# A state-space layer and an MLP on one core: the same operations in a newly found order, and one memset in 32-bit words

## The chip, the cores and the metric

The kernel runs on one core of a Trainium2 chip. The metric is the device time of one execution in microseconds (us). The core has a matrix engine (TensorE, "PE" in the profile; its weight loads are shown as "PEld"), a vector engine (VectorE, "DVE"), a scalar engine (ScalarE, "ACT") and a general engine (GpSimd, "POOL"). SyncE ("SP") issues nearly all DMA transfers. Each engine works through its own instructions in the order in which they are written, and waits for others by semaphores. So an instruction that waits holds up all that stands behind it on its engine.

## The reference

```
x  = A_u                                     # 1 x 2048 x 512, bf16
h  = x + A(layernorm(x))                     # state-space convolution
h2 = h + B(layernorm(h))                     # MLP 512 -> 1376 -> 512

A:  dt = exp(log_dt);  logdA = dt*(A_re + i A_im)       # 512 x 128
    K[d, l] = Re sum_n C[d,n] * exp(logdA[d,n]*l) * dt*B[d,n]     # l = 0..2047
    y = irfft(rfft(pad(K)) * rfft(pad(u)))[:2048] + u * Dskip
B:  y = layernorm(x);  gelu(y @ w1 + b1) @ w2 + b2      # with the tanh form of gelu
```

The position `l` is rounded to bf16 in the reference, and the kernel follows that rounding with masks.

## The kernel before

The 2048 positions are two blocks of 1024 (b = 0, 1), the 512 channels four column groups of 128 (c = 0 to 3). The stages, in the order in which the work mostly runs:

- **Front.** GpSimd fills small tables of constants with many small memsets (`fld_fn`, `cv_fn`, `cv3_fn`, `cod_fn`), VectorE and ScalarE make rates, angles and sizes from the parameters (`Front.rates`, `angles`, `size`, `side`, `phase`; helpers `TS`, `STT`, `TT` with lines 565 to 584, ScalarE's `AC` with line 591). `restack` and `phase` send small pieces through DMA to other partitions. This is done for two halves of the channels, c = 0, 1 and c = 2, 3.
- **Tables.** `aexps` and `bexps` make exponentials. `chain` (lines 985 to 1010) and `chain1` (lines 1019 to 1031) keep an angle in PSUM, to which TensorE adds a step; ScalarE takes its sine (lines 1000, 1029), and VectorE multiplies it into the tables EA, EB, IA and IB (lines 1010, 1031).
- **Kernel samples.** `kgen` (lines 1049 to 1068) makes K from the tables of one c by many small matmuls, 33 columns each, in half-groups of 5 or 6 indices. `kspec` and `kspec1` put K into order, write it to DRAM (AK_d for c = 0, 1; AKc_d for c = 2 and c = 3) and read it back in another layout; `fstage` (line 940) makes the spectrum. `ktail` and `klate` do the later half of K through AL_d.
- **Input.** `load_u` brings the input block (eight DMAs of 128 KB each block), `lnorm` normalizes it (bn_stats on line 899, scaling on line 906), `austage` (line 919) and `xspec` transform it.
- **Inverse.** `inverse` multiplies spectra on VectorE (line 1193) and transforms back on TensorE (line 1203). `turn` (line 1219) turns a result over by a DMA transpose on SP; for c = 3 of the first block TensorE does it (line 1212).
- **MLP.** `tail` adds the residual, normalizes twice and turns the result for the MLP (lines 1273 to 1305). `mlp` runs `w1` (line 1321, gelu on ScalarE, line 1323), `w2` (line 1337) and the last add (line 1339) for four pieces of 512 positions, and stores them.

Copies out of PSUM go through `evac` (ScalarE on line 517, VectorE on line 519), and each may be given to either engine. Everything lies in one SBUF arena, so every tile is called `ar` in the profile, and every PSUM tile `ps`.

The code first lists 1094 operations (`Sched.add`, with an engine, a planning cost, what is read and written) and then emits them in the order of the list `ORDER`. An entry k stands for operation k//2, and k%2 says which of its engines runs it. A negative entry -1-z puts one fill matmul on TensorE that writes PSUM bank z and is read by nobody (line 1434, in `fill`). `SLOTS` gives the PSUM banks in the same order. The costs, the `hv` numbers and the functions `c_act` and `c_dve` were used by the planner that found ORDER; when the kernel is built they have no effect. The order of ORDER alone fixes each engine's queue, SP's DMAs included.

Of the kernel before, what the change touches and what calls it, by code (L numbers as in the profile page):

```python
# [13 lines left out]
i32 = mybir.dt.int32  # L14
# [168 lines left out]
class VS(V):  # L183
# [59 lines left out]
]  # L243
SLOTS = "01012012034626026502020244602624062662062604046020262604064202462704264026024602460264206406204602467024602745020120415701425601624024672303642074350501246210675460165323401613712360172314231041502310"


TURN = 450000


class Sched:  # L250
    def __init__(self):
        self.ops = []
        self.wr, self.rd = {}, {}
        self.pr = 0.0
# [82 lines left out]
def c_act(n, ptr=0):  # L337
    return max(0.12, 0.055 + n / 1200.0) + (0.0, 0.09, 0.225, 0.225)[ptr]


def c_dve(n, mode=1, psum=False):
    return (0.08 if n < 64 else 0.065) + n / mode / 960.0
# [3 lines left out]
def kernel(ctx, tc, A_u, A_A_re, A_A_im, A_B_re, A_B_im, A_C_re, A_C_im, A_log_dt, A_Dskip,  # L346
# [4 lines left out]
    class Pe:  # L351
        n, dry, act, md = 0, True, 0.0, []
# [220 lines left out]
    def TT(o, a, b, op, n=None, mode=1, psum=False, oap=None, aap=None, bap=None, pr=None, eng="DVE"):  # L573
# [3 lines left out]
        if op == ALU.pow:  # L577
            c["POOL"] = 0.6 + 0.19 * n
# [907 lines left out]
```

## Time and profile before

| | us |
|---|---|
| median of 3 runs | 243.34 (242.45 to 243.55) |
| the profiled execution, whole time | 245.59 |
| its span, first to last instruction | 243.2 |
| TensorE busy | 215.4 (89%) |
| VectorE busy | 179.6 (74%) |
| ScalarE busy | 170.5 (70%) |
| GpSimd busy | 18.3 (8%) |

The granted clock of TensorE was 0.999 over the span. The chain of work that ended last is 59% TensorE, 26% VectorE, 5% DMA, 4% "issue" (time in which an engine waited for nothing that the profile shows) and 3% SP's queue. A row for a group of instructions gives line, engine, operation, shapes and number, then busy time, the mean of one in ns, and the idle time before them with what ended it. A row of a timeline gives start, length and the same names, with idle time before it in brackets. A row for a stretch of time gives, after its bounds and length, the busy time and the number of instructions for PE, PEld, DVE, ACT and POOL, then the granted clock, the share of the DMA engines' time, and GB/s.

### The profile page before, as it was taken

What the parts mean: (1) busy time and instruction counts of PE and PEld (TensorE: products, weight loads), DVE (VectorE), ACT (ScalarE), POOL (GpSimd) and SP (SyncE); (2) the same over time, 40 slices, a digit from 0 to 9 for tenths busy, and PEclk for the clock granted to TensorE, in tenths of its full rate; (3) what the DMA queues carried; (4) which work ended last, traced back from release to release, by engine and by line L of the source; (5) the groups of instructions that cost most, each with busy time, mean ns of one, the idle gap of its engine ahead of it and who ended that gap; (6) DMA issues with size and microseconds to landing.
All of it is one profiled execution on the core that took longest, in us unless ns stands there. A gap on an engine that the chain in (4) does not pass through costs nothing.

```text
span 243.2 us, 8615 instructions
## 1 busy us (share of the span) xinstructions
PE 215.4 (89%) x3696; PEld 126.2 (52%) x3705; DVE 179.6 (74%) x407; ACT 170.5 (70%) x232; POOL 18.3 (8%) x145
## 2 busy tenths in 40 slices
PE   7559786878988876979998999999999999999994
PEld 2436243656634454755775476655554444444443
DVE  6999999999999995659998988797506991213022
ACT  3999999999999956975997987785134402903700
POOL 8800000011000000300000010010000101000000
PEclk9999999999999999999999999999999999999999
DMA  5121124000013943417899485644514051142303
GB/s 149 34 62 44 38 19 82 20 3 7 3 25 82 214 132 125 125 30 163 231 159 210 121 254 95 214 80 85 99 28 83 0 106 27 41 88 65 86 19 71
DMA packets 42448, 21.40 MB, mean 88 GB/s; under 512 B 30761, under 2 KB 40618, under 8 KB 42410
## 3 DMA queue, kind: packets, MB, share of 16 engines
q1 hardware_dynamic: 42250, 20.79, 38.0%
q8 instruction: 29, 0.48, 0.8%
q10 hardware_dynamic: 160, 0.07, 0.1%
q14 instruction: 9, 0.07, 0.1%
HBM read 10.33 MB, written 4.49 MB: 61 GB/s over the span
## 4 chain that ended last, share of the span: by engine, by line
PE 59%; DVE 26%; DMA 5%; issue 4%; SPq 3%; ACT 1%; DVEq 0%; ACTq 0%
PE ps L1321 16%; PE ps L1337 16%; PE ps L1203 7%; DVE ar L579 5%; DVE ar L519 4%; DMA ar<-ar 4%; PE ps L919 4%; PE ps L940 3%; DVE ar L1010 3%; SPq L530 3%; DVE ar L584 3%; PE ps L1054 3%; DVE ar L1031 3%; PE ps L1278 3%; PE ps L1055 2%
## 5 line engine op out<-in xcount | busy, mean ns | idle before, releaser
L517 ACT CAST ar<-ps 128x1024 bf16<-128x1024 f32 (+4 forms) x66 | 59.0, 941 | 16.7 <-PE ps L1203 7.5
L1323 ACT ACTIVATE ar<-ps,ar 128x512 bf16<-128x512 f32 (+1 forms) x44 | 27.6, 686 | 35.3 <-PE ps L1321 35.3
L1321 PE MATMUL ps<-ar 128*128 128x512 bf16 (+1 forms) x176 | 39.8, 379 | 0.0
L1337 PE MATMUL ps<-ar 128*128 128x512 bf16 (+2 forms) x179 | 38.5, 366 | 0.6 <-issue 0.3
L1339 DVE TENSOR_TENSOR ar<-ps,ar 128x512 bf16<-128x512 f32 (+1 forms) x17 | 10.8, 657 | 36.1 <-PE ps L1337 32.7
L519 DVE CAST ar<-ps 128x1024 bf16<-128x1024 f32 (+5 forms) x29 | 29.2, 1015 | 8.9 <-ACT ar L1029 2.8
L1193 DVE TENSOR_TENSOR ar<-ar 128x1024 bf16<-128x1024 bf16 x48 | 30.7, 685 | 6.5 <-PE ps L1203 6.0
L1337 PEld LDWEIGHTS <-ar 128*128 128x128 bf16 (+1 forms) x187 | 18.0, 98 | 19.6
L1321 PEld LDWEIGHTS <-ar 128*128 128x128 bf16 (+1 forms) x176 | 17.2, 100 | 20.4 <-issue 1.0
L1054 PE MATMUL ps<-ar 128*20 128x33 bf16 x512 | 20.0, 249 | 6.1 <-issue 5.6
L1203 PE MATMUL ps<-ar 64*128 64x128 bf16 x768 | 23.7, 216 | 0.1
L1203 PEld LDWEIGHTS <-ar 64*128 64x128 bf16 x768 | 21.5, 94 | 4.3 <-issue 2.1
L1029 ACT ACTIVATE ar<-ps 128x1024 bf16<-128x1024 int16 x20 | 19.6, 1039 | 3.0 <-issue 2.4
L579 POOL TENSOR_TENSOR ar<-ar 128x4 f32<-128x4 f32 (+1 forms) x6 | 7.4, 1226 | 187.5 <-DVE ar L584 149.3
L1010 DVE TENSOR_TENSOR ar<-ar 128x1024 bf16<-128x1024 bf16 x32 | 21.2, 684 | 0.2
L1055 PEld LDWEIGHTS <-ar 128*20 128x20 bf16 x512 | 17.7, 125 | 6.5 <-issue 6.4
L1055 PE MATMUL ps<-ar 128*20 128x33 bf16 x512 | 20.1, 248 | 0.0
L1054 PEld LDWEIGHTS <-ar 128*20 128x20 bf16 x512 | 17.6, 124 | 3.0 <-DVE ar L1031 1.5
L723 ACT ACTIVATE ar<-ar 128x512 bf16<-128x512 f32 x32 | 18.2, 628 | 0.5 <-DVE ar L565 0.5
L919 PE MATMUL ps<-ar 128*32 128x512 bf16 x256 | 15.7, 380 | 1.4 <-ACT ar L517 0.6
L1027 PE MATMUL ps<-ar 128*32 128x256 f16 (+2 forms) x288 | 13.5, 280 | 2.8 <-ACT ar L1029 2.7
L1031 DVE TENSOR_TENSOR ar<-ar 128x512 bf16<-128x512 bf16 x40 | 15.4, 413 | 0.3
(99 smaller groups left out, 284.6 us busy)
## 6 DMA issues: line engine op xcount, KB each, us to landing
ar<-in_A_u_dram SPq DMA_DIRECT2D x16, 128.0 KB
ar<-in_A_u_dram SPq DMA_DIRECT2D x8, 256.0 KB
out_dram<-ar SPq DMA_DIRECT2D x30, 64.0 KB
ar<-in_B_w_dram SPq DMA_DIRECT2D x4, 344.0 KB
ar<-in_B_w_dram SPq DMA_DIRECT2D x2, 640.0 KB
AK_d<-ar SPq DMA_DIRECT2D x2, 512.0 KB
ar<-AK_d SPq DMA_DIRECT2D x2, 512.0 KB
AKc_d<-ar SPq DMA_DIRECT2D x4, 256.0 KB
```

The costliest lines, as they stand in the source:

```text
L517: act.copy(out_fn(), in_fn())
L519: dve.tensor_copy(out_fn(), in_fn())
L919: pe.matmul(pst(p)[32 * j:32 * j + 32, 512 * z:512 * z + 512], lhsT=BX.ap()[:, f0 + z, 16 - 16 * c:48 - 16 * c], rhs=src[2 * j + c].ap(), ...
L1010: add("DVE", c_dve(1024, 2), lambda e, lo=lo, rv=rv, sz=sc[z], e0=e0, o0=o0, q=q: dve.tensor_tensor(ent(o0, q, lo, 4, rv), ent(e0, q, lo, ...
L1031: add("DVE", c_dve(512, 2), lambda e, sc=sc, b0=b0, tb=tb, z=z: dve.tensor_tensor(tb[b0:b0 + 4].ap(), EA[c][b0:b0 + 4].ap(), sc[z].ap(), A ...
L1054: pe.matmul(o, lhsT=Ar.ap()[:, :, d], rhs=Br.ap()[:, :, d], start=True, stop=False, tile_position=(0, 32 * g))
L1055: pe.matmul(o, lhsT=Ai.ap()[:, :, d], rhs=Bi.ap()[:, :, d], start=False, stop=True, tile_position=(0, 32 * g))
L1193: dve.tensor_tensor(o, a, b_[:, :, ::-1, :] if sw else b_, ALU.mult)
L1203: pe.matmul(pst(p)[:, 512 * h + 128 * k:512 * h + 128 * k + 128], lhsT=q.ap()[rows, 2 * k + r, :], rhs=TP[w].ap()[rows, f0 // 2 + k, :], s ...
L1321: pe.matmul(pst(p)[:fs], lhsT=w1s[dc].ap()[:, fc * P:fc * P + fs], rhs=ybuf.ap().rearrange("p (t c) k -> p c t k", c=4)[:, dc], start=(dc ...
L1323: add("ACT", c_act(512, 1), lambda e, p=p, fc=fc, fs=fs: act.activation(hT.ap()[:fs, fc, :], pst(p)[:fs], ACT.Gelu_apprx_tanh, bias=b1_sb. ...
L1337: pe.matmul(pst(p)[:, c0:c1], lhsT=hT.ap()[:fs, fc, 128 * t:128 * t + 128], rhs=w2s[fc].ap()[:fs, c0:c1], start=(fc == 0), stop=(fc == NFC ...
```

## The change

The operations and their arithmetic stay. One memset of VectorE, of the value 256.0 in 16-bit floats over 2048 elements of one partition, is written as 1024 32-bit words that hold the same bits. Planning costs and `hv` numbers of several operations are altered. ORDER and SLOTS are replaced by newly found ones.

```
-    add("DVE", 0.3, lambda e: dve.memset(HLs.part(64, 65).ap().rearrange("p c g d -> p (c g d)"), 256.0), w=[HLs.part(64, 96)], pr=0.5)
+    add("DVE", 0.95, lambda e: dve.memset(HLs.part(64, 65).ap().rearrange("p c g d -> p (c g d)").bitcast(i32), 0x5C005C00), w=[HLs.part(64, 96)], pr=0.5)

 def c_act(n, ptr=0):
-    return max(0.12, 0.055 + n / 1200.0) + (0.0, 0.09, 0.225, 0.225)[ptr]
+    return max(0.12, 0.1 + n / 1200.0) + (0.0, 0.09, 0.2, 0.2)[ptr]
...
-            c["POOL"] = 0.6 + 0.19 * n
+            c["POOL"] = 0.37 + 0.16 * n
...
 ORDER = [
-    94, 396, 382, 386, 78, 380, 0, 284, 72, 30, 32, 100, 2, 98, 38, 40, 96, 228, 4, 146, 42, 310, 138, 44, 76, 282, 102, 8, 200, 104, 300, 110, 118,
...
-    2136, 2138, 2178, 2180, 2162, 2160, 2148, 2164, 2182, 2166, 2186, 2168, 2170, 2150, 2184, 2172, 2174,
+    0, 78, 94, 310, 386, 30, 32, 384, 382, 96, 100, 2, 38, 98, 4, 146, 228, 68, 8, 6, 40, 198, 312, 138, 300, 54, 102, 266, 314, 302, 12, 104, 118,
...
+    2160, 2138, 2170, 2174, 2136, 2180, 2182, 2172, 2186, 2184,
 ]
-SLOTS = "01012012034626026502020244604262...
+SLOTS = "01232013450262626242240244636404...
```

Decoded, the two orders differ in these places, among others:

| queue | before | after |
|---|---|---|
| SP, start | all six parameter loads and log_dt, one u load, then restacks and u loads mixed | four parameter loads and log_dt, small bias and Dskip loads between the other two, then restacks, most u loads of block 0 behind them |
| SP, middle | 8 u loads of block 1, 2 AK_d writes, AK_d read, AL_d write, AK_d read, AL_d write | 2 AK_d writes, AK_d read, 8 u loads of block 1, AK_d read, 2 AL_d writes |
| SP, next | AL_d reads and 3 loads of x, then 4 AKc_d writes, 4 AKc_d reads, first `turn` | an AL_d read, the first large `w2` load, AL_d reads and 1 load of x among the first two AKc_d writes, 2 AKc_d reads, 2 more writes, first `turn`, 2 more AKc_d reads |
| VectorE, start | 13 operations ahead of the first product of `rates` (line 579) | 10 |
| TensorE, fill matmuls | 11, 8, 6 and 3 ahead of `kgen` for c = 2, 10 in the first `tail` | 8, 6 and 3, and 10 |
| TensorE | last `austage` group of block 0 and a late step of `chain1` behind the first half-groups of `kgen` for c = 2 | ahead of it |
| `lnorm` of block 0 | among the first sines of `chain1` | behind most table products of c = 0, 1 |
| GpSimd | `select` ahead of the large iota of the front | last of the early work |

36 copies and scalings change between ScalarE and VectorE: 19 to VectorE, 17 to ScalarE.

More of the change, by code (lines that the diff above doesn't have):

```diff
@@ L199 @@
 ORDER = [
[43 rows of a table removed]
[43 rows of a table added]
 ]
-SLOTS = "01012012034626026502020244602624062662062604046020262604064202462704264026024602460264206406204602467024602745020120415701425601624024672303642074350501246210675460165323401613712360172314231041502310"
+SLOTS = "01232013450262626242240244636404042626042602602624624202046204622046702460206426042640240264026402640236042364704504675467360247014026452601412632464563701670356071234725360125601205321642405601340102"
 TURN = 450000
@@ L567, in fn @@
                 en.tensor_scalar(a, b, f(s1), f(s2), op0, op1)
-        add(eng, max(c_dve(n, mode, psum), 0.15 if isinstance(s1, V) else 0.0) if eng == "DVE" else 0.25 + n / 1540.0, fn, r=r, w=[o], pr=pr, hv=1)
+        add(eng, max(c_dve(n, mode, psum), 0.15 if isinstance(s1, V) else 0.0) if eng == "DVE" else 0.25 + n / 1540.0, fn, r=r, w=[o], pr=pr, hv=3 if mode == 4 else 2)
     def PTS(o, i, s1, s2=1.0, op0=ALU.mult, op1=ALU.mult, **k):
@@ L638, in fld_fn @@
                 gp.memset(t_.ap()[:, n:n + 1], v_)
-    POOL(2.0, fld_fn, w=[fi, fsh, fmk, fm, fa], pr=0.05, hv=1)
+    POOL(2.0, fld_fn, w=[fi, fsh, fmk, fm, fa], pr=0.05, hv=2)
     TT(fi, fi, fsh, ALU.logical_shift_right, pr=0.1)
@@ L654 @@
     codT = at(X0[8].lo, i32, 16, 2, 64)
-    POOL(1.1, lambda: gp.iota(iT.ap(), pattern=[[4, 16], [64, 64]], base=1, channel_multiplier=0), w=[iT], pr=0.6)
+    POOL(1.1, lambda: gp.iota(iT.ap(), pattern=[[4, 16], [64, 64]], base=1, channel_multiplier=0), w=[iT], pr=0.6, hv=1)
     for rp in range(2):
@@ L659 @@
     TS(oh, i1, q5, None, ALU.is_equal, pr=0.3)
-    POOL(0.2, lambda: gp.memset(cst.ap(), 256.0), w=[cst], pr=0.1)
+    POOL(0.5, lambda: gp.memset(cst.ap(), 256.0), w=[cst], pr=0.1, hv=1)
     for cs in range(2):
@@ L680, in cv_fn @@
                 gp.memset(hv.ap()[:, n:n + 1], float(h_))
-    POOL(1.3, cv_fn, w=[cv, hv], pr=0.2, hv=1)
+    POOL(0.72, cv_fn, w=[cv, hv], pr=0.2, hv=2)
     cv3 = ct(f32, NA)
@@ L686, in cv3_fn @@
             gp.memset(cv3.ap()[:, a:a + 1], LA[a] - 0.5)
-    POOL(1.0, cv3_fn, w=[cv3], pr=0.25, hv=1)
+    POOL(0.67, cv3_fn, w=[cv3], pr=0.25, hv=2)
     W3 = tL(f16, NA, 32)
@@ L848, in cod_fn @@
             gp.memset(cod.ap()[:, n:n + 1], v)
-    POOL(0.8, cod_fn, w=[cod], pr=0.3, hv=1)
+    POOL(0.5, cod_fn, w=[cod], pr=0.3, hv=2)
     TT(cod, cod, fi, ALU.logical_shift_right, bap=lambda: fi.ap()[:, 11:12].to_broadcast([P, 15]), pr=0.8)
@@ L1127, in sel @@
                 gp.affine_select(out=a, in_=a, pattern=[[-16 * st_, NJ // st_ + (st_ - 1) * (NJ % 2)], [-1, 2]], compare_op=ALU.not_equal, fill=1.0, base=-2 * m, channel_multiplier=1)
-        POOL(3.6, sel, w=[Selw], hv=1)
+        POOL(3.9, sel, w=[Selw])
         p = Ps(n=1)
```

82 rows, old and new, of the table ORDER are left out of this document.

## The prediction

> **What bounds the kernel now.** I read the page first, then stretches of time, then the waits of TensorE, then its timeline beside that of the DMA queue.
>
> ```profile
> span 243.2 us, 8615 instructions
> ...
> PE 215.4 (89%) x3696; PEld 126.2 (52%) x3705; DVE 179.6 (74%) x407; ACT 170.5 (70%) x232; POOL 18.3 (8%) x145
> ...
> q8 instruction: 29, 0.48, 0.8%
> ...
> 0.00:5.20 5.20, 3.80 (x12) 1.18 (x12) 3.37 (x13) 1.70 (x2) 4.54 (x92) 1.00 0.49 138
> 5.20:85.20 80.00, 63.49 (x1418) 38.62 (x1416) 78.80 (x210) 78.49 (x113) 7.60 (x50) 1.00 0.24 51
> 85.20:243.20 158.00, 148.14 (x2268) 86.37 (x2277) 97.46 (x185) 90.32 (x118) 6.19 (x6) 1.00 0.46 105
> 239.84:243.20 3.36, 0.01 (x1) 0.00 (x0) 0.42 (x1) 0.00 (x0) 0.00 (x0) 0.94 0.27 59
> ```
>
> The last four lines are stretches: length, then busy time (and instructions) of PE, PEld, DVE, ACT and POOL, granted clock, DMA share, GB/s. No engine is the bound throughout. From 5.2 to 85.2 us VectorE works 78.8 of 80.0 us, ScalarE 78.5, and TensorE has 16.5 us to spare. At 85.2 the first `kgen` matmul for c=2 starts, and from there TensorE works 148.1 of 158.0 us. So the span is three things: when VectorE has finished the tables of c=2, how much TensorE work is left then, and the 9.9 us in which TensorE stands still after that. Of those, 3.4 are the last add and store. The next fence has most of the rest.
>
> ```profile
> PE ps L1054 <- issue: 4.5, 3, 1.8
> ...
> 88.25 0.27 PE L1054 MATMUL ps<-ar 128*20 128x33 bf16 x4 [1.62 <-issue]
> ...
> 94.17 0.27 PE L1054 MATMUL ps<-ar 128*20 128x33 bf16 x4 [1.83 <-issue]
> ...
> 106.73 0.27 PE L1054 MATMUL ps<-ar 128*20 128x33 bf16 x4 [1.01 <-issue]
> ...
> 88.24:94.16 5.92, 4.09 (x128) 2.81 (x128) 5.41 (x12) 3.86 (x4) 0.00 (x0) 1.00 0.67 200
> 94.16:106.72 12.56, 11.54 (x384) 8.69 (x384) 7.02 (x20) 11.18 (x13) 2.16 (x2) 1.00 0.27 77
> ```
>
> Three pauses in `kgen`, for no data ("issue"), together 4.5 us. Between the first two TensorE ran 128 matmuls and 128 weight loads, 256 instructions; between the second and the third 768, three times as many. The page's instruction queue moved 29 packets, and 7,401 TensorE instructions over 29 are 255. So the pauses sit where a new packet of 256 instructions begins. Whether a packet is late is seen beside the transfers:
>
> ```profile
> 74.05 1.87 SPq L530 DMA_DIRECT2D ar<-in_A_u_dram  x3
> ...
> 76.60 3.74 SPq L530 DMA_DIRECT2D ar<-in_A_u_dram  x5
> 80.44 1.16 SPq L530 DMA_DIRECT2D AK_d<-ar  x2
> 88.12 0.34 SPq L530 DMA_DIRECT2D ar<-AK_d  x1
> ...
> 89.03 0.41 SPq L530 DMA_DIRECT2D ar<-AK_d  x1
> ...
> 82.00:85.80 3.80, 3.76 (x104) 2.24 (x99) 3.77 (x12) 3.80 (x6) 0.00 (x0) 1.00 1.15 274
> 85.80:88.00 2.20, 0.83 (x52) 0.70 (x41) 2.20 (x6) 1.03 (x2) 0.00 (x0) 1.00 0.18 50
> 88.00:92.00 4.00, 3.75 (x124) 2.65 (x126) 4.00 (x8) 2.70 (x3) 0.00 (x0) 1.00 0.64 175
> ```
>
> While the u loads and the two spectrum writes (AK_d) drain, the DMA engines are over 100% busy, and TensorE starts again at 88.25, 2.45 us after they fell idle at 85.8; the second pause lies in the spectrum reads (88 to 92).
>
> **The change part by part.** The altered costs, hold numbers and caps enter only the planner; the order is written out, so they add no instruction and cost 0. What runs differently is the memset, ORDER, SLOTS and the engine of 36 evictions and scalings.
>
> *The memset.*
>
> ```profile
> 0.91 0.38 DVE L1356 MEMSET ar<- 128x384 uint32 x1
> ...
> 2.03 1.76 DVE L670 MEMSET ar<- 1x2048 f16 x1 [0.46 <-issue]
> ...
> 5.21 0.42 DVE L579 TENSOR_TENSOR ar<-ps,ar 128x256 f32<-128x256 bf16 x1 [0.15 <-ACT ar L591]
> 5.67 1.33 DVE L565 TENSOR_SCALAR ar<-ar 128x256 f32<-128x256 f32 x2
> ...
> 8.61 0.29 DVE L567 TENSOR_SCALAR ar<-ar 128x256 f32<-128x256 f32 x1
> ```
>
> 2,048 elements take 1.76 us; 1,024 words, by the 384 that take 0.38, about 1.0. The 0.8 saved are worth nothing: VectorE waits for ScalarE's first exponential until 5.21 in either case. If that cover were gone they would be worth 0.8.
>
> *VectorE up to the tables of c=2.* Counted in the two orders. Ahead of the add at 5.21 now stand 0.6 us less of small work (the BX memset of 0.38, three more memsets and two 14-element steps go behind it; a cast, a memset and an EB memset come ahead); it must be done later: +0.6. Ahead of the last table product of c=2, evictions change engine: three of 1024 columns, one of 330 and three of 256 come to VectorE, two of 1024 and one of 256 leave.
>
> ```profile
> L519 DVE CAST ar<-ps 128x1024 bf16<-128x1024 f32 x3 | 3.6, 1216 | 0.0
> L519 DVE CAST ar<-ps 128x330 bf16<-128x330 f32 x1 | 0.5, 495 | 0.0
> L519 DVE COPY ar<-ps 128x256 bf16<-128x256 bf16 x1 | 0.4, 418 | 0.0
> ```
>
> That is 1.2 + 0.5 + 2 x 0.4 = 2.5, 2.2 after neighbours' overlap. Against it: the two scalings at 5.67 took 1.33 us where such a one takes 0.29 at 8.61; they ran beside GpSimd's row of small memsets, which stands elsewhere now. Of the 0.75 lost I take back 0.5 (0 to 0.75; other scalings may meet the memsets). VectorE's own waits in this stretch, 80.0 - 78.8 = 1.2, I halve (0 to 1.2), as its queue holds more work that depends on TensorE's early results: -0.6. Sum: 0.6 + 2.2 - 0.5 - 0.6 = +1.7; `kgen` of c=2 would start at 86.9.
>
> *TensorE's work left then.* One `austage` group and one chain step come ahead of that `kgen`:
>
> ```profile
> 82.94 0.86 PE ps L919 x16
> 83.81 0.43 PE ps L1027 x8
> ...
> 141.29 2.33 PE L1434 MATMUL ps<-ar 128*128 128x512 bf16 x10
> ```
>
> 0.86 + 0.3 (the step moved is a short one) = -1.15. The fill matmuls ahead of it fall from 28 to 17. By the ten at 141.29 eleven are 2.6 us, but they stand in the 16.5 us that TensorE has to spare: 0; without that cover a gain of 2.6. The ten later fills stay.
>
> *The queue of SP beside the packets.* Before, eight u loads, two spectrum writes, and both spectrum reads once those have landed. After: the writes go ahead of the u loads, then one read, the eight u loads, the other read. Worked from their producers, the writes would issue near 73, the first read near 78 and the u loads until about 83.5, so all is drained near 87, when TensorE is only about to enter `kgen`. The packet boundaries hardly move in the code (22 fill instructions fewer, 48 moved ahead: 26 instructions on, still in the second and fourth half-group of `kgen`). So the packet for the first pause comes beside u loads and the second beside nothing: of 1.62 + 1.83 = 3.45 I keep 0.5 (bounds 0 and 3.45): -2.95.
>
> *The third pause.* It came beside loads of x:
>
> ```profile
> 100.45 1.18 SPq L530 DMA_DIRECT2D ar<-in_A_u_dram  x2
> ...
> 149.90 1.82 SPq L530 DMA_DIRECT2D ar<-in_B_w_dram  x2
> ```
>
> After, the first large w2 load (640 KB, before at 149.90) issues here, as soon as `kgen` of c=2 has freed its place, and the first AKc write and an x load follow: two boundaries are in reach. I take 2.0 for 1.0 (bounds 0 and 4.2, the second being 640 KB at 274 GB/s, 2.4 us, and 1.83 for the other): +1.0.
>
> *From the inverse on.* Turns (L1219) and tails keep their order, but the reads for the last spectrum (c=3) now stand behind the first turn on SP. I put 0.3 on it; its worst is a rival below. The out stores have no reader: 0. The last add and store are the same two halves in the other order: 0. The first-half u loads, moved behind the restacks, are read by `lnorm`, which itself moves some 8 us later: 0. The bre load waits behind two tiny loads; the transposes that read it stand behind other work: 0 (0 to 0.5).
>
> Sum: 1.7 - 1.15 - 2.95 + 1.0 + 0.3 = -1.1. The profiled run took 245.59 for its span of 243.2, 2.2 above the median 243.34; differences are the same in both, so 243.34 - 1.1 = 242.2.
>
> **The rivals.**
>
> *All pauses go.* The w2 load may miss the boundaries by a microsecond. Then 1.7 - 1.15 - 4.5 = -3.9: 239.4. For it: in the 12.56 us from 94.16 two of three boundaries passed without a pause beside x loads. Against: 640 KB is more than any of these.
>
> *The pause moves to the w2 load (other side).* Place: the boundaries in `kgen` c=3. Price 4.2 there, and 1.0 left at the first: 1.7 - 1.15 - 4.45 + 5.2 + 0.3 = +1.6: 244.9. It decides from 4.8 us of pauses on, above which the change is slower by 0.5%.
>
> *The last spectrum waits behind the turn (other side).*
>
> ```profile
> 111.80 4.43 PE ps L919 x80
> ...
> 119.56 3.10 SPq L1219 DMA_TRANSPOSE ar<-ar  x1
> ...
> 115.16 2.55 SPq L530 DMA_DIRECT2D ar<-AKc_d  x4
> ...
> 122.45 1.03 PE ps L940 x32
> ```
>
> Between the second inverse group and that spectrum TensorE has 9.6 us of work (five L919 groups are 4.43 of it). The eviction (1.2), the turn (3.1), two issues (0.8) and, from the end of the issues to the use as before, 4.7 (117.7 to 122.45) make 9.8; if the reads also queue behind the transposes' data, another 2 to 3. A wait of 3.1 in place of 0.3 gives 245.0; it decides from 2.6.
>
> *The pauses have nothing to do with the transfers.* They would stay: 1.7 - 1.15 + 0.3 = +0.9: 244.2, no change that can be told. For it: a boundary with idle DMA would have to pause too, and in the 12.56 us two did not; so I give it little. [...]
>
> **How the numbers follow.** 0.5% is 1.2 us, about what a measurement here can tell. Forecast (241 to 243.5 as its own range): 0.45, of which 0.25 lies below 242.1 and 0.20 within. All pauses go 0.15, faster. Pause at w2 0.17 and wait behind the turn 0.15, slower. Pauses untouched 0.08, same. So faster 0.40, same 0.28, slower 0.32. The range runs from below the first rival, 239.2, to 246.0, a microsecond over the slow ones, since VectorE's +1.7 reaches +2.8 with no wait saved.
>
> **What would show it.** Right: `kgen` of c=2 starting 1 to 3 us later than 85.2; TensorE's waits with "issue" on L1054 below 3 us; AK_d writes issued before the u loads, near 73; VectorE idle in 0 to 5.2 growing from 1.8 to about 3.4. Wrong: L1054 pauses of 4.5 or more, a wait of L940 on a DMA near 120, or VectorE waiting for u loads in L899 near 90.

## The result, and the profile after

The changed kernel takes 250.56 us (median of 4 runs, 248.88 to 251.61); the kernel before, run beside it, 243.27 (242.45 to 243.55). The ratio is 1.030, 95% interval 1.023 to 1.037: 3% slower, where 242.2 was forecast, and outside the range of 239.2 to 246.0.

First the page of the changed kernel: span, engines (busy time, share, instructions) and TensorE's granted clock in 40 slices of 6.2 us, each digit in tenths of full speed (9 is 90% or more).

```profile
span 249.6 us, 8578 instructions
...
PE 218.5 (88%) x3685; PEld 125.8 (50%) x3694; DVE 180.1 (72%) x409; ACT 171.4 (69%) x230; POOL 19.3 (8%) x145
...
PEclk9967799999995899988999999999999999999999
```

This execution took 251.42. Its span is 6.4 us longer than the 243.2 of before, with nearly the same busy time on every engine: the time went into waiting. The clock line is new. Before, it was 1.00 in every stretch quoted but the last 3.4 us; now it has two dips, near 20 us (0.50 from 16 to 20) and near 78 (0.50 from 76 to 80), and a shallow one near 110 (0.77 from 108 to 112).

Next, stretches of the changed kernel, cut at its first `kgen` matmul for c=2 (94.27 instead of 85.22); columns as in the prediction, the granted clock third from the end.

```profile
5.20:94.27 89.07, 66.72 (x1431) 38.38 (x1429) 82.22 (x219) 79.28 (x109) 8.07 (x69) 0.90 0.24 53
94.27:249.60 155.33, 147.98 (x2244) 86.29 (x2253) 94.50 (x181) 89.97 (x118) 6.60 (x6) 0.99 0.49 103
...
72.00:76.00 4.00, 1.23 (x16) 0.41 (x16) 3.91 (x5) 1.74 (x3) 0.00 (x0) 1.00 0.09 17
76.00:80.00 4.00, 3.69 (x36) 1.26 (x39) 3.30 (x7) 2.94 (x4) 0.00 (x0) 0.50 0.45 133
80.00:84.00 4.00, 4.00 (x72) 1.93 (x64) 3.85 (x6) 2.01 (x3) 0.00 (x0) 0.64 0.46 135
```

The whole loss lies ahead of that point: +9.05 there, -2.7 after it (155.33 for 158.0). Of the 9.05, VectorE's work is 82.22 - 78.80 = 3.4, and its waits are 89.07 - 82.22 = 6.85 instead of 1.2, so 5.65. The prediction had +2.3 for the work (0.6 + 2.2 - 0.5) and -0.6 for the waits.

Which waits they are, VectorE's list to 95 us says (total, count, longest), and the timeline of three engines shows the first of them at work.

```profile
DVE ar L1010 <- ACT ar L591: 2.4, 1, 2.4
DVE ar L1031 <- ACT ar L1029: 1.8, 2, 1.3
DVE ar L519 <- PE ps L919: 0.8, 1, 0.8
```

```profile
67.28 4.66 ACT L1000 ACTIVATE ar<-ps 128x1024 bf16<-128x1024 int16 x5
...
69.30 0.42 DVE L584 SCALAR_TENSOR_TENSOR ar<-ar 128x256 f16<-128x256 f32 x1
...
71.80 0.26 ACT L591 ACTIVATE ar<-ar 128x32 f32<-128x32 int16 x1
...
72.09 1.29 DVE L1010 TENSOR_TENSOR ar<-ar 128x1024 bf16<-128x1024 bf16 x2 [2.37 <-ACT ar L591]
...
75.03 1.22 DVE L519 CAST ar<-ps 128x1024 bf16<-128x1024 f32 x1
75.23 1.94 ACT L1000 ACTIVATE ar<-ps 128x1024 bf16<-128x1024 int16 x2 [2.26 <-DVE ar L1010]
...
76.31 1.90 PE L1084 MATMUL ps<-ar 20*128 20x512 bf16 x16 [2.67 <-DVE ar L519]
```

VectorE has done its L584 at 69.72 and then stands until 72.09. It does not wait for a sine (L1000, in hand since 67.28) but for a 0.26 us activation of L591, 32 columns wide, that is queued behind five sines. Then the wait goes round: ScalarE loses 2.26 us to VectorE's product, TensorE 2.67 to VectorE's eviction, and its clock falls to 0.50 and 0.64 in the 8 us after. An L1084 and an L919 group of 16 matmuls, at 76.31 and 78.13, take 1.90 us each; in the kernel before an L919 group of 16 takes 1.05 (at 81.46), an L1084 group 1.04 (72.22).

Two theories could explain this. CLOCK: the missing fill matmuls, whose removal I costed at nothing, let the clock fall, and slow tables make everyone wait. ORDER: one wait in the new order comes first, and the clock only follows.

### The profile page after: what moved, and what is told of

It reads as the page before. It is cut to its first block, busy times and chain, and to the rows that moved or that the text cites. A ratio compares the mean times of both kernels' runs of the same rounds, so it can differ in the third digit from the quotient of the medians.

```text
span 249.6 us, 8578 instructions
## 1 busy us (share of the span) xinstructions
PE 218.5 (88%) x3685; PEld 125.8 (50%) x3694; DVE 180.1 (72%) x409; ACT 171.4 (69%) x230; POOL 19.3 (8%) x145
## 4 chain that ended last, share of the span: by engine, by line
PE 55%; DVE 3%; DMA 2%; ACT 2%; issue 1%; POOL 1%; SPq 1%; DVEq 0%; ACTq 0%
PE ps L1321 15%; PE ps L1337 15%; PE ps L1203 8%; PE ps L940 3%; PE ps L919 3%; PE ps L1278 2%; PE ps L1054 2%; DMA ar<-AKc_d 2%; PE ps L1055 2%; PE ps L1109 2%; DVE ar L519 1%; ACT ar L1029 1%; PE ps L1169 1%; POOL ar L579 1%; DVE ar L1010 0%
## 5 line engine op out<-in xcount | busy, mean ns | idle before, releaser
L517 ACT CAST ar<-ps 128x1024 bf16<-128x1024 f32 (+4 forms) x68 | 60.0, 939 | 16.7 <-issue 5.4
L1321 PE MATMUL ps<-ar 128*128 128x512 bf16 (+1 forms) x176 | 40.5, 379 | 0.0
L1337 PE MATMUL ps<-ar 128*128 128x512 bf16 (+3 forms) x179 | 38.8, 366 | 0.5 <-issue 0.2
L519 DVE CAST ar<-ps 128x1024 bf16<-128x1024 f32 (+5 forms) x27 | 26.9, 1006 | 6.6 <-PE ps L940 2.1
L1054 PE MATMUL ps<-ar 128*20 128x33 bf16 x512 | 19.7, 249 | 2.9 <-issue 2.0
L1029 ACT ACTIVATE ar<-ps 128x1024 bf16<-128x1024 int16 x20 | 19.6, 1029 | 2.9 <-PE ps L1027 1.9
L1055 PE MATMUL ps<-ar 128*20 128x33 bf16 x512 | 19.7, 248 | 0.3 <-issue 0.3
L1054 PEld LDWEIGHTS <-ar 128*20 128x20 bf16 x512 | 17.5, 124 | 3.3 <-issue 1.9
L1000 ACT ACTIVATE ar<-ps 128x1024 bf16<-128x1024 int16 x16 | 15.2, 1035 | 3.4 <-DVE ar L1010 2.3
L919 PE MATMUL ps<-ar 128*32 128x512 bf16 x256 | 17.1, 409 | 0.3
L1031 DVE TENSOR_TENSOR ar<-ar 128x512 bf16<-128x512 bf16 x40 | 15.6, 421 | 2.0 <-ACT ar L1029 1.8
## 6 DMA issues: line engine op xcount, KB each, us to landing
ar<-in_A_u_dram SPq DMA_DIRECT2D x8, 256.0 KB, 4.4
AKc_d<-ar SPq DMA_DIRECT2D x4, 256.0 KB, 3.2
```

The source lines that it names most:

```text
L517: act.copy(out_fn(), in_fn())
L519: dve.tensor_copy(out_fn(), in_fn())
L919: pe.matmul(pst(p)[32 * j:32 * j + 32, 512 * z:512 * z + 512], lhsT=BX.ap()[:, f0 + z, 16 - 16 * c:48 - 16 * c], rhs=src[2 * j + c].ap(), ...
L1029: add("ACT", c_act(1024), lambda e, sc=sc: act.activation(sc.ap().rearrange("p z a b -> p (z a b)"), pst(p, i16).rearrange("p (n two) -> p ...
L1054: pe.matmul(o, lhsT=Ar.ap()[:, :, d], rhs=Br.ap()[:, :, d], start=True, stop=False, tile_position=(0, 32 * g))
L1055: pe.matmul(o, lhsT=Ai.ap()[:, :, d], rhs=Bi.ap()[:, :, d], start=False, stop=True, tile_position=(0, 32 * g))
```

## The experiments

All twelve, with the start of `kgen` for c=2 in the profiled execution. Ratios are against runs of the kernel before on the same chip in the same session (medians 243.2 to 243.7). The intervals reach 0.4 to 0.8% to either side, so two rows that lie 1 us apart are not told apart.

| Kernel | Median us | Ratio, 95% interval | `kgen` c=2 from |
|---|---|---|---|
| before | 243.3 | 1 | 85.2 |
| changed | 250.56 | 1.030 (1.023 to 1.037) | 94.3 |
| e1 small activation later | 245.77 | 1.010 (1.003 to 1.018) | 89.7 |
| e7 the two entries swapped | 245.54 | 1.011 (1.005 to 1.017) | 88.6 |
| e2 changed, early fills | 250.33 | 1.028 (1.020 to 1.036) | 94.0 |
| e3 changed, fills in the gap | 249.04 | 1.023 (1.016 to 1.029) | 91.9 |
| e4 before, without 11 fills | 243.22 | 0.999 (0.995 to 1.003) | 85.4 |
| e5 as e1, evictions' engines as before | 250.24 | 1.026 (1.021 to 1.032) | 92.9 |
| e9 as e7, four evictions back | 245.28 | 1.011 (1.007 to 1.016) | 88.3 |
| e6 before, new order on SP | 246.09 | 1.012 (1.007 to 1.017) | 85.4 |
| e8 before, profiled again | 245.45 (one run) | | 85.4 |
| e10 before, 32-bit memset | 243.42 | 0.999 (0.995 to 1.003) | 85.2 |
| e11 as e7, w2 load later | 245.08 | 1.010 (1.006 to 1.014) | 88.4 |
| e12 e9 and e11 together | 245.06 | 1.011 (1.006 to 1.017) | 88.9 |

**e1: the small activation later.** The edit, in ORDER (entry 762 is the L591 activation, 880 VectorE's product, 934 the first sine of `chain1`):

```diff
-  ..., 728, 744, 762, 880, 742, ...
+  ..., 728, 744, 880, 742, ...
-  ..., 1104, 1106, 1118, 934, ...
+  ..., 1104, 1106, 1118, 762, 934, ...
```

> The changed kernel with one ScalarE instruction moved: the 128x32 activation of L591 (0.26 us at 71.80), which stood between the chain's sines, goes behind two evictions, just ahead of the first sine of chain1. Theory ORDER (VectorE's chain products at 72.09 waited 2.37 us for this one small instruction, and all of TensorE's idle 2.67 us at 73.64 and its halved clock from 76 to 84 follow from that): the wait is gone, the granted clock stays at 1.00 from 70 to 90, kgen of c=2 starts 3 to 5 us earlier than 94.27, time 245.5 to 248. Theory CLOCK (the tables are slow because TensorE runs at a low clock that the missing fill matmuls no longer hold up): VectorE's wait only moves to the next sine, the clock still falls, gain under 1 us: 249.5 to 250.5.

245.77, 4.8 us less than the changed kernel; 89.7 instead of 94.3. ORDER, as it said. It does not yet say whether the activation's place on ScalarE costs this, or the wait for it.

**e7: the two entries swapped.**

```diff
-  ..., 744, 762, 880, ...
+  ..., 744, 880, 762, ...
```

> The changed kernel with two neighbouring entries of ORDER swapped: the small ScalarE activation of L591 (entry 762) is now written out behind VectorE's chain product of L1010 (entry 880) instead of ahead of it. Every engine runs the same instructions in the same order as in the changed kernel; only a wait between these two can differ, since both touch the one arena tile. Theory FALSE WAIT (the product waits for the activation only because that is written out first, though the planner lists no dependency between them): VectorE's wait of 2.37 us goes, ScalarE's activation does not wait either, and the time falls as in the run before this, by 4 to 5 us to 245.5-246.5. Theory PLACE (the activation's place on ScalarE's queue, 0.26 us ahead of the last sine, is what costs): no change, 250 to 251.

245.54. The same timeline, and stretches, of this kernel:

```profile
66.90 4.66 ACT L1000 ACTIVATE ar<-ps 128x1024 bf16<-128x1024 int16 x5
...
68.91 0.42 DVE L584 SCALAR_TENSOR_TENSOR ar<-ar 128x256 f16<-128x256 f32 x1
...
69.25 1.29 DVE L1010 TENSOR_TENSOR ar<-ar 128x1024 bf16<-128x1024 bf16 x2
...
71.42 0.26 ACT L591 ACTIVATE ar<-ar 128x32 f32<-128x32 int16 x1
```

```profile
5.20:88.61 83.41, 64.54 (x1432) 38.38 (x1434) 81.79 (x218) 78.80 (x109) 8.64 (x69) 0.94 0.25 58
88.61:243.30 154.69, 148.56 (x2257) 86.13 (x2253) 94.25 (x181) 89.75 (x118) 6.60 (x6) 0.99 0.49 103
...
76.00:80.00 4.00, 3.76 (x100) 1.99 (x96) 3.93 (x7) 3.89 (x5) 0.00 (x0) 1.00 0.72 208
```

Every engine's instructions are the same and in the same order, the activation still stands behind five sines, and yet the product follows the L584 at once. So the wait was no need of the data: the planner's list of dependencies has no entry between the two. In the program as built the changed kernel's product waits for the activation, and with the entries swapped for an earlier instruction of ScalarE, the sine whose values it reads.

The addresses say where the two meet. Counted in 2-byte elements of a partition of the arena tile, the product writes two runs of 512, from 64800 and from 69024; the activation reads between 66688 and 66750 and writes 67584 to 67647. No element is shared, but all of the activation lies in the gap between the two runs. That the wait is put there because the whole range from the first run to the end of the second counts as written is inferred from this, not tested. Of 7 us of loss this one neighbourhood in a list costs 5.0 (250.56 - 245.54).

**e2 and e3: fills put back into the changed kernel.** e2 has them where the clock first fell, e3 where TensorE waits 2.67 us (entry 1100 is that L1084 group).

```diff
 e2:  -7, -7, -7, -7, -7, -7, -7, -7, 242, ... -4, -4, -4, -4, 332, ...
 e3:  -8, -8, -8, -8, -8, -8, -8, -8, 1100, ...
```

> The changed kernel with 12 fill matmuls (L1434) more: 8 ahead of the L790 step that waits from 13.6 to 15.5, 4 ahead of the first L964 group at 18.06. Nothing else differs. Theory CLOCK: the granted clock from 12 to 28 rises from 0.5-0.8 to 1.00, the chain's first matmul comes before 24.3 instead of 24.58 and everything to 60 us runs 1 to 1.5 us earlier; time down by 1 to 2 us, to about 249. Theory ORDER: the clock rises too, but VectorE and ScalarE were busy 23.1 and 21.5 of 24.3 us in that stretch, so under 0.5 us is gained.

> The changed kernel with 8 fill matmuls (L1434) ahead of the L1084 group that waits from 73.6 to 76.3. Nothing else differs. Theory CLOCK: TensorE stays busy in the gap, the granted clock from 76 to 84 stays at 1.00 instead of 0.50 and 0.64, the L1084, L919 and L1027 groups there take 1.0 instead of 1.9 us, and kgen of c=2 starts 2 to 3 us earlier: 247.5 to 248.5. Theory ORDER: the waits of VectorE and ScalarE stay where they are, only TensorE's slack changes: gain under 1 us.

In e2's profile the clock is whole in the early part (two stretches of the changed kernel, then of e2), and its time is the same:

```profile
12.00:16.00 4.00, 1.49 (x15) 0.77 (x18) 3.93 (x17) 3.77 (x9) 0.00 (x0) 0.82 0.15 37
16.00:20.00 4.00, 2.86 (x45) 1.85 (x45) 3.89 (x14) 3.47 (x6) 0.00 (x0) 0.50 0.25 61
```

```profile
12.00:16.00 4.00, 2.69 (x14) 1.54 (x13) 3.96 (x18) 3.50 (x9) 0.00 (x0) 1.00 0.21 52
16.00:20.00 4.00, 3.83 (x53) 1.73 (x54) 3.86 (x12) 3.28 (x8) 0.00 (x0) 1.00 0.23 56
```

From 16 to 20 TensorE at half clock is busy 2.86 of 4 us, and VectorE 3.89 and 3.86: the early dip costs nothing that these runs can tell (250.33 for 250.56). That the fills kept the clock up there is not shown, since e1 and e3, without them, have 1.00 from 16 to 20 too. The later dip stays in e2, 0.50 from 76 to 80. e3 gained 1.5 us by the medians (249.04), between what the two theories gave. VectorE's wait for the activation is still there, 2.4 us, and the clock from 76 to 84 is 1.00:

```profile
76.00:80.00 4.00, 4.00 (x81) 1.84 (x82) 4.00 (x8) 3.68 (x5) 0.00 (x0) 1.00 0.47 133
```

VectorE's waits in L1031 for sines (L1029), 1.8 us in the changed kernel and 1.7 in e2, are 0.2 in e3: this is where the slow clock reached it. So of the 5.0 us of this wait about 1.5 are paid through the clock after it, and the rest by the wait and what follows from it. The 1.5 is an estimate: the runs of the two kernels overlap (247.75 to 249.61, 248.88 to 251.61).

**e4: the kernel before without its 11 fills** (`-5` eleven times ahead of entry 406, taken out).

> The kernel before, without its 11 fill matmuls at 21.86 to 24.4. Nothing else differs. This is the step that I costed at nothing. Theory CLOCK: TensorE idles 2.2 us there, the granted clock falls to 0.5 to 0.8 in the next microseconds, the chain's matmuls take 1.0 instead of 0.6 us, and the time rises by 1.5 to 3 us to 245-246. Theory ORDER: the fills cover nothing that matters: 243.3, within 0.5.

243.22, ratio 0.999. The step that I costed at nothing is worth nothing; CLOCK falls as a first cause. The clock did not even dip without them: it is 1.00 in every stretch of 4 us from 8 to 32 us. So e4 does not show what a dip there would have cost.

**e5 and e9: the moved evictions.** e7 is still 2 us above the kernel before. Entries of ORDER are twice the operation's number plus the engine's index, so one digit moves an eviction (0 ScalarE, 1 VectorE):

```diff
e5, on e1
-  207 208 641 643 1097 1113 1104 851 862 838 843 867
+  206 209 640 642 1096 1112 1105 850 863 839 842 866
e9, on e7
-  207 641 643 1097
+  206 640 642 1096
```

> The changed kernel with the small activation moved (as in the first experiment, 245.77 us) and with the 12 evictions ahead of kgen of c=2 that had changed engine put back on the engine of before; every place in the order stays. Theory WORK (the rest of the loss, 245.77 against 243.68, is VectorE's busy time, 82.6 us after 78.8 before, of which the moved evictions are 2.5): VectorE is busy 80 to 80.5 us to the same point, kgen of c=2 starts near 87.3 instead of 89.68, time 243 to 244. Theory BALANCE (ScalarE then becomes the later one: it had 79.7 busy of 84.5 us and gets 2.3 more): VectorE waits for ScalarE's sines instead, the gain is under 1 us, 245 to 246.

> The changed kernel with the two entries swapped (245.54 us), and besides with only four of the moved evictions back on ScalarE: the three of 256 columns before 26 us and the one of 330 columns near 65. The large ones stay on VectorE. Theory WORK (VectorE's busy time ahead of kgen of c=2 sets its start, and early on ScalarE has room: 21.5 busy of 24.3 us): VectorE has 1.7 us less to do (3 x 0.42 + 0.49), kgen of c=2 starts 1.2 to 1.7 us earlier than 88.6, time 244 to 244.5. Theory BALANCE (any work given to ScalarE comes back as VectorE's wait for it): start at 88.5 or later, 245.5 to 246.5.

Stretches to `kgen` of c=2, of e5 and of e9:

```profile
5.20:92.89 87.69, 66.30 (x1432) 38.82 (x1431) 81.68 (x218) 80.93 (x115) 9.05 (x69) 0.92 0.29 63
```

```profile
5.20:88.30 83.10, 64.34 (x1432) 37.98 (x1434) 80.55 (x215) 80.36 (x114) 9.08 (x69) 0.98 0.26 57
```

In e9 VectorE's work falls by 1.2 (81.79 to 80.55) and its waiting grows by 0.9 (1.6 to 2.55), so the start moves by 0.3 only. That is close to BALANCE, and the time is the same as e7's within what the runs tell apart. e5 lies outside both theories: VectorE waits 6.0 us, 2.4 of it in L1031 for sines, and the kernel loses 4.5. ScalarE is not full there, 80.93 of 87.69 us; its own longest wait is 2.2 for TensorE, and the granted clock is 0.92. Why e5 loses so much stays open. So the moved evictions could not be taken back in the two ways tried. That VectorE's extra work, 3.0 us in e7, makes up the 2 us that remain fits the later start of `kgen` (88.6 for 85.2), but no run has shown it by removing it.

**e6 and e8: the pauses.** e6 puts the new order of SP's middle part into the kernel before:

```diff
-  u loads x8, AK_d write x2, AK_d read, AL_d write, AK_d read, AL_d write
+  AK_d write x2, AK_d read, u loads x8, AK_d read, AL_d write x2
```

> The kernel before with one part of the change alone: on SP's queue the two AK_d writes and the read that needs only them go ahead of the eight u loads, and the other read behind these. All other queues as before. Theory PACKETS (the issue pauses of L1054 come from instruction packets beside the u loads and AK_d transfers): the pauses near 86.6 and 92.3 shrink from 3.45 to under 1 us in the profile and the median falls by 1 to 3 us, to 240.5-242.5. Theory NO LINK: the pauses stay or only vary from run to run, median within 0.7 of 243.5.

> The kernel before, unchanged, profiled once more. The profile my sum was made on had a span of 243.2 us and 4.5 us of issue pauses in L1054, while unprofiled runs of the same kernel had spans of 239.7 to 242.7. Theory VARIES (the pauses differ from run to run and the first profile showed a bad one): a span of 240 to 241.5 with 1.5 to 3 us of pauses. Theory FIXED: 4 to 5 us of pauses again whatever the span.

e6 is slower by 1.2%, which neither theory gave. Its timeline and stretches show the long pause beside full DMA engines that the new order was to avoid; the third fence is the DMA engines' busy share from 93 to 94.5, each digit 0.0375 us in tenths:

```profile
80.47 5.93 SPq L530 DMA_DIRECT2D ar<-in_A_u_dram  x8
...
86.93 0.12 PEld L1055 LDWEIGHTS <-ar 128*20 128x20 bf16 x1 [0.24 <-issue]
...
93.44 0.69 DVE L899 BATCH_NORM_STATS2 ar<-ar 128x6 f32<-128x512 bf16 x1 [5.28 <-DMA AL_d<-ar]
...
95.59 0.28 PE L1054 MATMUL ps<-ar 128*20 128x33 bf16 x4 [4.57 <-issue]
```

```profile
84.00:88.00 4.00, 3.86 (x128) 2.54 (x124) 3.96 (x11) 3.10 (x5) 0.00 (x0) 1.00 1.12 136
88.00:92.00 4.00, 3.02 (x104) 2.01 (x93) 0.16 (x1) 3.79 (x4) 0.00 (x0) 1.00 1.15 139
92.00:96.00 4.00, 0.41 (x23) 0.41 (x26) 2.56 (x6) 0.00 (x0) 0.00 (x0) 0.62 0.41 108
```

```profile
DMA  9999999999996334111411101000000111201101
```

From 84 to 92 the DMA engines are over-full (1.12 and 1.15); they stay full until 93.45 and are nearly idle from 93.6 on. TensorE stands from 91.02 to 95.59, 4.57 us of "issue" in the middle of `kgen`, and goes on about 2 us after they have drained. Its program is that of the kernel before, and the pause has the place of the one at 94.17 there, ahead of which stand 1,628 matmuls and 1,629 weight loads: the rows behind the two are the same. It is 4.57 us long here, beside a DMA share of 1.15 from 88 to 92, and 1.83 there, beside 0.64. At the place of the pause at 88.25 there (1.62 us; 72 matmuls behind the first of `kgen` in both), a weight load waits 0.24 us here (86.93), with the DMA share at 1.12 from 84 to 88. So over-full DMA engines went with a long pause at one of the two places only. VectorE waits 5.28 us beside the long pause, in the L899 that reads the u tiles, which now come later. Which of the two waits the 2.4 us of the medians (246.09 - 243.69) come from was not separated. In the kernel before `kgen` starts at 85.4, and the later u loads run straight into it. The changed kernel and e7 start it later and have no pause beside the u loads; that the new order of SP is good for them is not tested alone.

e8 is the kernel before once more, and e10 and e4 have the same code from there on. TensorE's issue waits in e8 and in e10, and e10's stretch from `kgen` on:

```profile
PE ps L1054 <- issue: 2.0, 2, 1.2
```

```profile
PE ps L1054 <- issue: 1.4, 1, 1.4
```

```profile
85.19:239.50 154.31, 148.49 (x2277) 86.40 (x2277) 97.21 (x185) 90.39 (x118) 6.19 (x6) 1.00 0.47 108
```

VARIES for the pauses: 2.0 and 1.4, not 4.5. The profile that I argued from had 9.9 us of idle TensorE behind 85.2, e10 has 5.8 with the same program there, and e4 takes 154.32 us from there on, as e10 does. The span that VARIES gave, 240 to 241.5, was missed: in e8's 243.6 the stretch from `kgen` on is 158.18 us for e10's 154.31, with TensorE busy 151.45 for 148.49 and a granted clock of 0.81 from 100 to 110 and 0.85 from 110 to 120, where e10 has 1.00 over the whole.

**e10: the memset alone** (1,024 words of 0x5C005C00 for 2,048 f16 elements of 256.0, in the kernel before).

> The kernel before with the memset of HLs in 1,024 32-bit words instead of 2,048 f16 elements, and nothing else. Theory IDLE COVERS IT: the memset falls from 1.76 to 0.9 us, VectorE then waits that much longer for ScalarE's first exponential before its add at 5.21, and the time is the same within 0.5%: 243 to 244. Theory IT COUNTS: 0.8 us faster, 242.9 by the middle.

```profile
1.82 0.91 DVE L670 MEMSET ar<- 1x1024 int32 x1 [0.25 <-issue]
...
3.94 0.17 DVE L579 TENSOR_TENSOR ar<-ar 128x14 int32<-128x14 int32 x1 [0.84 <-POOL ar L638]
```

0.91 for 1.76, and VectorE waits 0.84 for GpSimd right behind it. 243.42, no change.

**e11 and e12: the first 640 KB w2 load** (entry 1406), from the middle of `kgen` to just ahead of its other half on SP; e12 adds the four evictions of e9.

```diff
-  1406 behind the first AL_d read
+  1406 ahead of 1408
```

> The changed kernel with the two entries swapped (245.54 us), and the first 640 KB w2 load moved back on SP's queue from the middle of kgen of c=2 and c=3 to just ahead of the other w2 half, as before. All other queues the same. Theory PACKETS (the pause of 1.28 us at 102.19 comes because the packet that began at 101.04 stood behind this load, which kept the DMA engines full from 99.5 to 101.3): the pause goes or falls under 0.4 us, time 244.3 to 245. Theory NO LINK: the pause stays near 1.3 us, 245.5.

> Both of the two kernels before this one together: four evictions back on ScalarE and the w2 load later. If both theories hold (WORK and PACKETS), their gains of about 1.3 and 1.0 us add up: 243 to 243.8, level with the kernel before. If BALANCE or NO LINK holds, 244.5 or more.

The row of e7, and the row of e11 that takes its place:

```profile
103.47 0.27 PE L1054 MATMUL ps<-ar 128*20 128x33 bf16 x4 [1.28 <-issue]
```

```profile
147.65 0.61 PE L1321 MATMUL ps<-ar 128*128 128x512 bf16 x2 [1.46 <-DMA ar<-in_B_w_dram]
```

The pause in `kgen` goes, as PACKETS has it, and in e11 a wait of 1.46 for weights comes at 147.65. The times did not follow: 245.08 against 245.54 is within what the runs tell apart, and e12 adds nothing (245.06). Against the gains that were expected, e11 lies just outside its range and e12 well outside. No version here beats the kernel before.

## Why the prediction was wrong, step by step

**The step that failed: "VectorE's own waits in this stretch, 1.2, I halve: -0.6".** They became 6.85 us, so the term was +5.65. I gave a general reason (more early TensorE results in the queue) and named no wait. The order has it in sight: entry 762 stands directly ahead of 880 and behind five sines. I had counted VectorE's instructions and the evictions that change engine, and never asked of the ScalarE instructions that move what is queued ahead of them and which VectorE instruction is written out behind them. e7 shows that one such pair is 5.0 of the 7.3 us between the medians (250.56 - 243.27). None of the four rivals had it either. What remains, about 2 us, is VectorE's extra work by the account below, which is argued and not shown.

**VectorE's work, +2.3: right in kind, short by about 1.** It came to +3.4 (3.0 in e7). The evictions are as counted: three of 1024, three of 256 and one of 330 columns more, two and one less, 2.5 us. The 0.5 that I took back for scalings that no longer meet GpSimd's memsets did not come in sum. By shape, twelve scalings of 256 columns (L565) take 0.6 us less, but other scalings stand beside GpSimd's memsets now (those from 4.99 to 7.22 us): eight of L567 take 2.68 us instead of 2.30, and one of 128x64 takes 0.48 instead of 0.19. The first row, of the changed kernel, holds this one and one of 256 columns; the second is the kernel before.

```profile
5.12 0.61 DVE L565 TENSOR_SCALAR ar<-ar 128x64 f32<-128x64 int32 x2
```

```profile
36.38 0.19 DVE L565 TENSOR_SCALAR ar<-ar 128x64 f32<-128x64 int32 x1
```

The small work that moved behind 5.2 us came to about 1.1 instead of 0.6: 1.3 for the BX memset, two memsets of L669 and one of L1382, two 14-element products and a small cast, less 0.2 for a scaling that moved ahead.

**TensorE's work left, -1.15: too large.** TensorE was busy 147.98 us behind the first `kgen` matmul for c=2, after 148.14, with 24 matmuls fewer as counted. The granted clock was 0.95 from 94 to 126; at 1.00 from `kgen` on, TensorE was busy 147.49 in e9 and 148.18 in e11, so what the clock has in it is not shown. **From the inverse on, +0.3: right.** TensorE waited 0.4 for the last spectrum.

**The pauses, -2.95: borne out at one place, size wrong.** In e6, where SP's order alone differs, TensorE stands 4.57 us at one of these places, beside DMA engines at 1.15, and hardly at the other (0.24), beside 1.12; that an instruction packet is what comes late is inferred from the counts of 256, and that the transfers make it late is inferred too, from the one place. I priced it from one execution that was 2.2 us above the median, and wrote that "differences are the same in both". They were not: the excess was in the pauses themselves, 4.5 us there and 1.4 and 2.0 in e10 and e8. The changed kernel has 1.3. From `kgen` of c=2 on, the changed kernel's 155.33 is 2.7 less than in that execution, near the -2.8 of my sum, and 1.0 more than e10's 154.31. The gain was real only against an unlucky run.

**The third pause, +1.0: the place was right, the price was not seen.** The w2 load does stand beside a pause of 1.28 us, and the pause goes with the load (e11), but the time does not fall by as much as the runs could tell.

**The fills, 0, and the memset, 0: right** (e4, e10). The first needs care all the same: the 11 fills of the kernel before are worth nothing, and 8 fills about 1.5 us in the one gap of 2.67 us that the false wait had opened (e3).

**What was to be seen.** In order: AK_d writes ahead of the u loads, yes, though all of it late.

```profile
76.74 3.81 SPq L530 DMA_DIRECT2D AK_d<-ar  x2
83.53 0.34 SPq L530 DMA_DIRECT2D ar<-AK_d  x1
86.99 5.11 SPq L530 DMA_DIRECT2D ar<-in_A_u_dram  x8
```

L1054 issue waits below 3 us, yes, 1.3 behind the first `kgen` matmul for c=2. `kgen` of c=2 1 to 3 us late, no, 9.05. VectorE's idle time in 0 to 5.2 grown to 3.4, no: it stayed at 1.8 (5.20 - 3.37), since a scaling that stood later now runs there, and takes 1.48 us beside 56 small memsets of GpSimd (1.90 to 3.81); in the kernel before it took 0.18 (last row):

```profile
0.00:5.20 5.20, 3.80 (x12) 1.17 (x12) 3.37 (x12) 2.12 (x4) 4.60 (x73) 1.00 0.47 128
```

```profile
2.38 1.48 DVE L565 TENSOR_SCALAR ar<-ar 128x128 f16<-128x128 bf16 x1
```

```profile
7.71 0.18 DVE L565 TENSOR_SCALAR ar<-ar 128x128 f16<-128x128 bf16 x1
```

Of the three signs named for a wrong forecast none appeared at its size; L940 waited 0.4 for a DMA, at 131.72. I had looked for the loss behind 85 us, and it lay ahead of it. `select` was also misplaced in the table ahead of the prediction: its GpSimd work runs from 61 to 65 us, behind the first power of the statistics, not among the early work; no wait names it. Had the false wait alone been absent, e7's 245.54 would have been inside the range by luck: a gain was forecast, and e7 is still 2 us slower than before.

## What to carry to other kernels

Where waits are inferred from the written order on a shared tile, go through every instruction that a new order moves, small ones first, and ask two things: what is queued ahead of it on its own engine, and which instruction of another engine is written out right behind it; a list of true dependencies does not answer the second. A write in two runs deserves a look at what lies in the gap between them. Before a stall is priced from a profile, compare that execution with the median of the runs: if it is slow, the stall is the first suspect for being slow only there (here 4.5 us of pauses in an execution 2.2 us above the median, 2.0 and 1.4 in e8 and e10). Work moved between two engines that are both 94 to 98% busy (e7, e9) was not a sum of durations: 1.2 us less work on VectorE came with 0.9 more waiting. So try it back in part before calling it a cost.

## What the runs showed of the hardware

The pauses of `kgen` were expected to be 1 to 2 us each beside transfers; in e6, with the DMA engines at 1.12 and 1.15 from 84 to 88 and 88 to 92 us, TensorE stood for 4.57 at one place and a weight load for 0.24 at the other (1.83 and 1.62 in the kernel before). In executions that run the same program from there on, the pauses are 4.5, 2.0 and 1.4 us in sum (the first profile, e8, e10).

The same instructions ran at different granted clocks. Up to 66 us e1 and e3 run the same instructions, and these are their stretches from 24 to 28:

```profile
24.00:28.00 4.00, 2.69 (x20) 0.71 (x20) 3.93 (x12) 3.62 (x5) 0.00 (x0) 0.65 0.16 37
```

```profile
24.00:28.00 4.00, 2.87 (x24) 0.71 (x20) 3.93 (x12) 3.66 (x5) 0.00 (x0) 1.00 0.15 36
```

0.65 and 1.00 in the same part of the same program (the stretches cut it at slightly different places, 20 and 24 matmuls). From 16 to 20 us both have 1.00, and the changed kernel, also with the same instructions there, 0.50. From 76 to 80 us, behind TensorE's wait of 2.67, the changed kernel has 0.50, and e3, with eight fill matmuls in that wait, 1.00. What sets the clock beyond this is not shown.
